# Forward columns of a spectral stage laid end to end in whole PSUM banks

## The chip, the cores and the metric

The kernel runs on one core of one Trainium2 chip. The metric is the device time of one execution in microseconds. Before the change the median of three runs is 1106.13 us (1106.01 to 1106.82). The profiled execution took 1106.58 us, and its span, from the first to the last instruction in the trace, is 1104.8 us.

## The reference, cut to what matters

```python
x  = A_u                                   # (1, 2048, 576)
xn = layernorm(x)
K  = einsum("dn,dnl,dn->dl", Cc, exp(dt*A*l), dt*Bc).real   # response, 576 x 2048
y  = irfft(rfft(xn, padded) * rfft(K, padded))[:2048] + xn * Dskip
out = x + y + silu(xn @ w1) @ w2           # w1: 576 x 4608, w2: 4608 x 576
```

So two branches share the normalised input: a long convolution over 2048 positions with a computed response (done through a transform), and a dense pair of matmuls with a SiLU between them.

## The kernel before, in words

**Dense branch.** `ffn` works in 36 blocks (two halves of the rows, nine chunks of 512 inner features, two blocks of 512 rows). A block has eight main steps: four `up` steps (14 matmuls of 512 columns each, lines 343 to 345) and four `down` steps (24 matmuls of 288 columns, line 369). The operands are split in a high and a low part, so three products stand for one. An `up` result leaves PSUM through ScalarE (`gf`, `gh`, lines 351 and 352) and VectorE (`gl`, line 354). A `down` result is added to `acc` by VectorE (line 373); its bank `po` comes from a pool of two, so a late addition holds up the next `down` step.

**The order of the work.** TensorE, VectorE and ScalarE each run their queue in order. The program gives the dense steps, and a generator `side` gives everything else. `weave` lets the side generator go on whenever the dense branch has reached the share of its 288 main steps that the generator yielded. Where the code says `behind(ins)`, the instructions traced inside come after `ins` on their engine's queue; `tc.high_priority()` puts an instruction ahead of others that are ready. The rest of the order is made by a scheduler when the program is built.

**The spectral stage.** It is the part of `side` between the marks 0.597 and 0.86, main steps 172 to 248, about 671 to 971 us in the trace. Sixteen pairs p of transform rows go through it; each pair has a response side and an input side.

- `load_k(p)`, `load_u(p)`, `load_m(p, i)` (lines 752 to 775) are issued on POOL's queue: the response's rows in five DMAs into `kw`, the input's rows into `u`, and two matrices, `m2` and `mm`. Most tiles have two buffers.
- `halves(p)` (line 777): VectorE's butterfly of the response, three instructions of 128x576 (lines 783 and 785), from `kw` into the tile `k`.
- `visit` (line 787): the forward transform of one side of one pair. Sixteen fp32 matmuls with 64 rows and 32 weight columns, on eight tile positions of the array (two row groups g, four column groups o), each over half of the 576 columns. Every fp32 matmul shows as two instructions, hence x32. The result takes the tile `psb`, four banks with one buffer, and uses 288 of 512 columns in each bank.
- `response(p)` (line 802) is a visit on `k`, a clear of the banks by ScalarE (line 817) and six turns per pair on ScalarE (lines 808 to 810) that make `ka` and `kb`.
- `inputs(p)` (line 819) is a visit on `u`, a clear into `ut`, and the complex product on VectorE: per half two full and two half-height instructions (lines 827 to 830), a cast on ScalarE (`yh`, line 833) and a subtraction on VectorE (`yl`, line 834).
- `back(p)` (line 836): 12 matmuls of 288 columns into the same `psb` tile (line 847), a clear into `yo`, and two stores to `d2` on POOL's queue.

After a start-up the loop at line 877 yields three times for each pair: `response(p+1)`, then `halves(p+2)` and `inputs(p+1)`, then `back(p)`, some 1.4 main steps apart. There are 32 visits and 16 returns. After the stage, `tail` loads the stored rows (`conv_load`, line 933, on SP's queue) and `add_conv` finishes the convolution.

Of the kernel before, what the change touches and what calls it, by code (L numbers as in the profile page):

```python
# [19 lines left out]
P = 128  # L20
L = 2048
D = 576
# [4 lines left out]
HD = D // 2  # L27
# [16 lines left out]
def kernel(  # L44
# [22 lines left out]
    nc = tc.nc  # L67
# [15 lines left out]
    d2 = dram.tile([32 * P, D], F32, name="d2")  # L83
# [66 lines left out]
    pins = {}  # L150

    def behind(ins):
        return tc.issue_after(ins) if ins is not None else nullcontext()
# [306 lines left out]
    kl = yp = pa = tail_at = None  # L460
# [282 lines left out]

    def spectral():

        uv = d1u.rearrange("(m p r) d -> p r m d", m=2, r=P)
        kv = d1k.rearrange("(m p r) d -> p r m d", m=2, r=P)
        cwt = kl.tile([P, 16, 3], F32, name="cwt", bufs=1)
        nc.sync.dma_start(cwt, cw)
        us, ks, mats, kab, ys = {}, {}, {}, {}, {}  # L750

        def load_u(p):
            t = kl.tile([P, 2, D], F32, tag="u", name="u")
            nc.gpsimd.dma_start(t, uv[p])
            us[p] = t

        def load_k(p):
            if p > 15:
                return
            w = kl.tile([P, 3, D], F32, tag="kw", name="kw")  # L760
            nc.gpsimd.dma_start(w[:, 0:2], kv[p])
            for r in range(4):
                nc.gpsimd.dma_start(w[32 * r:32 * r + 32, 2], kv[p, 32 * (r ^ 1):32 * (r ^ 1) + 32, 1])  # L763
            ks[p] = w

        def load_m(p, i):
            if p > 15:
                return
            if i:
                t = kl.tile([P, 2, 2, P], F32R, tag="mm", name="mm")  # L770
                nc.gpsimd.dma_start(t, cm23[:, p, 1:].rearrange("r (k w) c -> r k w c", w=2))
            else:
                t = kl.tile([P, P], F32, tag="m2", name="m2")
                nc.gpsimd.dma_start(t, cm23[:, p, 0])
            mats[p, i] = t

        def halves(p):
            if p > 15:
                return
            w, t = ks[p], kl.tile([P, 2, D], F32, tag="k", name="k", bufs=1)  # L780
            ks[p] = t
            c = cwt[:, p]
            nc.vector.scalar_tensor_tensor(w[:, 2], w[:, 2], c[:, 0:1], w[:, 1], op0=ALU.mult, op1=ALU.add)
            for m in range(2):
                nc.vector.scalar_tensor_tensor(t[:, m], w[:, 2], c[:, 1 + m:2 + m], w[:, 0], op0=ALU.mult, op1=ALU.add)  # L785

        def visit(p, t, name):

            banks = psb.tile([P, 2, 2, 512], F32, tag="psb", name=name)
            last = pins["pe"]  # L790
            for n, (h, g) in enumerate(((0, 1), (0, 0), (1, 1), (1, 0))):
                gs = slice(64 * g, 64 * g + 64)
                for o in range(4):
                    os = slice(32 * o, 32 * o + 32)
                    with tc.high_priority(), behind(last):
                        last = nc.tensor.matmul(banks[os, g, h, :HD], mats[p, 0][gs, os], t[gs, o % 2, h * HD:(h + 1) * HD],
                                                start=True, stop=True, tile_position=(64 * g, 32 * o),
                                                skip_group_check=True).ins
            pins["pe"] = last
            return banks  # L800

        def response(p):

            kas = [kl.tile([P, D], F32, tag="ka", name="ka") for _ in range(2)]
            clear(visit(p, ks.pop(p), "pk"), kas)
            for g in range(2):
                ka, kb = kas[g], kl.tile([P, D], F32, tag="kb", name="kb")
                nc.scalar.mul(kb[:64], ka[64:], -1.0)
                nc.scalar.copy(kb[64:], ka[64:])
                nc.scalar.copy(ka[64:], ka[:64])  # L810
                kab[2 * p + g] = ka, kb

        def clear(banks, dsts):

            with tc.high_priority():
                for g in range(2):
                    nc.scalar.copy(dsts[g].rearrange("p (h d) -> p h d", h=2), banks[:, g, :, :HD])

        def inputs(p):

            uts = [kl.tile([P, D], F32, tag="ut", name="ut") for _ in range(2)]
            clear(visit(p, us.pop(p), "pu2"), uts)
            for g in range(2):
                ka, kb = kab.pop(2 * p + g)
                y = kl.tile([P, D], F32, tag="y", name="y", bufs=1)
                y2 = kl.tile([P, D], F32, tag="y2", name="y2", bufs=1)
                nc.vector.tensor_mul(y, uts[g], ka)  # L827
                nc.vector.tensor_mul(y2[:64], uts[g][64:], kb[:64])
                nc.vector.tensor_mul(y2[64:], uts[g][:64], kb[64:])  # L829
                nc.vector.tensor_add(y, y, y2)  # L830
                ys[2 * p + g] = [kl.tile([P, D], F32R, tag=n, name=n, bufs=2) for n in ("yh", "yl")]
                yh, yl = ys[2 * p + g]
                nc.scalar.copy(yh, y)  # L833
                nc.vector.tensor_sub(yl, y, yh)

        def back(p):

            pb = psb.tile([P, 2, 2, 512], F32, tag="psb", name="pb")
            last = pins["pe"]
            for g in range(2):  # L840
                mk = mats[p, 1][:, g]
                parts = ys.pop(2 * p + g)
# [6 lines left out]
            yos = [kl.tile([P, D], F32, tag="yo", name="yo") for _ in range(2)]  # L849
            clear(pb, yos)  # L850
            for g in range(2):
                nc.gpsimd.dma_start(d2.rearrange("(p k) d -> k p d", k=32)[2 * p + g], yos[g])

        def load_u2(p):
            if p < 16:
                load_u(p)

        load_k(0)
        load_m(0, 0)
        load_u(0)  # L860
        yield 1.0
        with behind(pins["gh"]):
            halves(0)
        load_m(0, 1)
        load_m(1, 0)
        yield 1.03
        load_k(1)
        load_u(1)
        yield 1.05
        response(0)  # L870
        yield 1.07
        halves(1)
        yield 1.085
        inputs(0)
        load_k(2)
        yield 1.1
        for p in range(16):
            if p < 15:
                response(p + 1)
                load_m(p + 1, 1)  # L880
            load_k(p + 3)
            yield 1.1 + 0.9 * (3 * p + 1) / 48
            halves(p + 2)
            if p < 15:
                inputs(p + 1)
            load_u2(p + 2)
            yield 1.1 + 0.9 * (3 * p + 2) / 48
            back(p)
            load_m(p + 2, 0)
            yield 1.1 + 0.9 * (3 * p + 3) / 48  # L890


    order = iter((0, 1, 2, 3, 8, 9, 10, 11, 4, 5, 6, 7, 12, 13, 14, 15))
# [66 lines left out]

    def side():
        nonlocal s4, kl, yp, pa, tail_at, f1, vt, pss, psb, ps3
        marks = (0.13, 0.597, 0.86)
        tail_at = (0.91, 0.934, 0.967, 0.0072)
        with tc.tile_pool(name="kf", bufs=1) as kfp, tc.tile_pool(name="pss", bufs=3, space=PSUM) as pss, tc.tile_pool(name="ps3", bufs=1, space=PSUM) as ps3:
            for n in ("f", "phi"):
# [170 lines left out]
```

## Time and profile before

| | before |
|---|---|
| median of three runs | 1106.13 us |
| profiled execution | 1106.58 us |
| its span | 1104.8 us |
| busy: TensorE, VectorE, ScalarE, POOL | 1095.5, 891.6, 659.5, 136.2 us |
| stage 671 to 971 us: the same | 297.7, 227.8, 199.9, 79.1 us |
| granted TensorE clock in the stage | 1.00 |

The engines are named PE (TensorE's matmuls), PEld (its weight loads, which overlap the matmuls), DVE (VectorE), ACT (ScalarE), POOL (GpSimd) and SP (SyncE). A row of a group reads: line, engine, operation, out<-in, shape, count | busy us, mean ns of one | idle time of the engine just before, and what ended it. A row of a timeline reads: start in us, length in us, engine, line, operation, tiles, shape, count of instructions merged in it. A row of waits reads: who waited for whom, total us, times, longest. Matmuls are pipelined and their ends are modelled, so the starts say how fast TensorE goes on.

### The profile page before, as it was taken

To read this page: it belongs to the slowest core of one execution; us is meant where nothing else is said; L and a number is where in the kernel's file an instruction comes from. 1 tells how busy PE (TensorE), PEld (TensorE's weight loads), DVE (VectorE), ACT (ScalarE), POOL (GpSimd) and SP (SyncE) were. 2 spreads that over 40 slices of the span, in tenths; PEclk is the share of its full clock that TensorE was granted. 3 is DMA by queue.
4 is the path that set the end of the run, shared out by engine and by line. 5 is a ranking of instruction groups with operands and counts; after the bars stand their busy time and mean duration, and the time that the engine had idled before them with its cause. 6 is when DMAs were issued, how large, how long until landed. Compare 5 with 4: busy or idle time off the path is not lost.

```text
span 1104.8 us, 23941 instructions
## 1 busy us (share of the span) xinstructions
PE 1095.5 (99%) x9807; PEld 961.4 (87%) x9807; DVE 891.6 (81%) x1431; ACT 659.5 (60%) x1030; POOL 136.2 (12%) x241
## 2 busy tenths in 40 slices
PE   9999999999999999999999999999999999999998
PEld 7999998999889898999989988788878878899887
DVE  7799899999999999989999836786868768653343
ACT  4565457676776776767766644766666656732220
POOL 1100000000000000011000023323232231000011
PEclk9999999999999999999999999999999999999999
DMA  9745512524253425265754166555546453248563
GB/s 265 208 123 155 150 58 62 121 72 118 85 108 107 99 76 137 62 157 154 198 150 96 55 143 211 163 160 173 166 145 188 151 168 122 67 144 209 135 173 107
DMA packets 174142, 150.23 MB, mean 136 GB/s; under 512 B 112288, under 2 KB 143792, under 8 KB 173904
## 3 DMA queue, kind: packets, MB, share of 16 engines
q1 hardware_dynamic: 156544, 93.77, 32.9%
q0 software_dynamic: 16736, 54.07, 15.6%
q8 instruction: 77, 1.26, 0.5%
q10 hardware_dynamic: 752, 0.85, 0.3%
q14 instruction: 33, 0.27, 0.1%
HBM read 104.13 MB, written 44.61 MB: 135 GB/s over the span
## 4 chain that ended last, share of the span: by engine, by line
PE 80%; DVE 10%; DMA 4%; ACT 2%; POOL 1%; issue 1%; DVEq 0%; ACTq 0%; POOLq 0%
PE po L369 35%; PE ph L343 30%; PE kp L708 3%; DMA kw<-d1k 3%; PE ph L344 3%; PE ph L345 2%; PE z L723 2%; DVE y L829 1%; PE pb L847 1%; DVE y L830 1%; PE pu L171 1%; DVE k L785 1%; DVE acc L373 1%; POOL kw L763 1%; DVE y L827 1%
## 5 line engine op out<-in xcount | busy, mean ns | idle before, releaser
L369 PE MATMUL po<-w2h,gh 128*128 128x288 f32 x1152 | 340.2, 297 | 2.2 <-DVE acc L373 2.1
L369 PE MATMUL po<-w2l,gh 128*128 128x288 f32 x1152 | 337.2, 295 | 0.0
L369 PE MATMUL po<-w2h,gl 128*128 128x288 f32 x1152 | 336.4, 296 | 0.2 <-DVE gl L354 0.2
L369 PEld LDWEIGHTS po<-w2h,gh 128*128 128x128 f32 x1152 | 215.7, 188 | 19.9 <-issue 8.4
L369 PEld LDWEIGHTS po<-w2l,gh 128*128 128x128 f32 x1152 | 215.5, 188 | 6.7 <-issue 1.9
L369 PEld LDWEIGHTS po<-w2h,gl 128*128 128x128 f32 x1152 | 214.9, 188 | 2.9 <-issue 0.9
L351 ACT ACTIVATE gf<-ph 128x512 f32<-128x512 f32 (+1 forms) x146 | 85.8, 588 | 186.9 <-PE ph L345 168.7
L354 DVE TENSOR_TENSOR gl<-gf,gh 128x512 fp32r<-128x512 f32 (+1 forms) x148 | 98.6, 671 | 87.3 <-ACT gh L352 86.7
L373 DVE TENSOR_TENSOR acc<-po,acc 128x288 f32<-128x288 f32 x288 | 126.0, 451 | 47.6 <-PE po L369 46.0
L343 PE MATMUL ph<-xh,w1h 128*128 128x512 f32 (+1 forms) x584 | 159.5, 389 | 0.0
L343 PE MATMUL ph<-xh,w1l 128*128 128x512 f32 (+1 forms) x584 | 159.2, 387 | 0.0
L343 PE MATMUL ph<-xl,w1h 128*128 128x512 f32 (+1 forms) x584 | 159.0, 387 | 0.0
L343 PEld LDWEIGHTS ph<-xl,w1h 128*128 128x128 f32 x584 | 107.0, 188 | 22.0 <-issue 1.4
L343 PEld LDWEIGHTS ph<-xh,w1l 128*128 128x128 f32 x584 | 106.7, 188 | 20.3 <-issue 0.5
L343 PEld LDWEIGHTS ph<-xh,w1h 128*128 128x128 f32 x584 | 103.6, 188 | 17.9 <-issue 0.9
L352 ACT CAST gh<-gf 128x512 fp32r<-128x512 f32 (+1 forms) x148 | 89.3, 610 | 19.4 <-PE po L369 16.4
L174 POOL DMA_DIRECT2D d1u<-u x32 | 17.4, 545 | 462.3 <-ACT u L173 460.4
L667 ACT ACTIVATE c<-th 128x1040 f32<-128x1040 f32 x36 | 38.7, 1075 | 46.0 <-DVE th L666 46.0
L833 ACT CAST yh<-y 128x576 fp32r<-128x576 f32 x32 | 21.5, 673 | 74.2 <-DVE y L830 71.0
L665 ACT ACTIVATE c<-th,magic 128x1040 f32<-128x1040 f32 x36 | 42.1, 1169 | 26.4 <-DVE C L688 23.3
L305 DVE TENSOR_TENSOR w1l<-w1r,w1h 128x640 fp32r<-128x640 f32 x72 | 57.0, 819 | 0.2
L344 PE MATMUL ph<-x,w1h 128*128 128x512 f32 (+1 forms) x146 | 56.6, 388 | 0.0
(195 smaller groups left out, 1757.7 us busy)
## 6 DMA issues: line engine op xcount, KB each, us to landing
w2r<-in_B_w_dram SPq DMA_DIRECT2D x72, 288.0 KB, 3.8
w1r<-in_B_w_dram SPq DMA_DIRECT2D x35, 512.0 KB, 3.9
d1u<-u POOLq DMA_DIRECT2D x32, 288.0 KB, 3.0
d1k<-stage SPq DMA_DIRECT2D x36, 256.0 KB, 5.1
u<-d1u POOLq DMA_DIRECT2D x16, 576.0 KB, 4.6
kw<-d1k POOLq DMA_DIRECT2D x16, 576.0 KB, 4.6
d<-yo POOLq DMA_DIRECT2D x32, 288.0 KB, 3.0
ys<-d SPq DMA_DIRECT2D x32, 288.0 KB, 6.0
```

The source lines that it names most:

```text
L305: pins["w1l"] = nc.vector.tensor_sub(l1, src, h1).ins
L343: nc.tensor.matmul(ph, w[:, kt, :], v[:, kt, a:e], start=n + kt == 0, stop=False)
L344: nc.tensor.matmul(ph, h1[:, 4, :], x4[:, a:e], start=False, stop=False)
L345: pins["pe"] = nc.tensor.matmul(ph, l1[:, 4, :], x4[:, a:e], start=False, stop=True).ins
L351: nc.scalar.activation(gf, ph, AF.Silu)
L352: pins["gh"] = nc.scalar.copy(gh, gf).ins
L354: pins["gl"] = nc.vector.tensor_sub(gl, gf, gh).ins
L369: pins["pe"] = nc.tensor.matmul(po[:, :HD], G[blk, t][g][:, js], W2[half, c, t][w][:, hs], start=n == 0, stop=n == 3 * FT - 1).ins
L373: nc.vector.tensor_add(acc[j][:, hs], po[:, :HD], acc[j][:, hs])
L665: nc.scalar.activation(c65, th, AF.Identity, bias=magic)
L667: nc.scalar.activation(c65, th, AF.Abs)
L708: mm = nc.tensor.matmul(dst, t[:, ch, :32], t[:, ch, 32:], start=begins and n == 0, stop=True, tile_position=(0, 32 * q), skip_group_check ...
```

## The change

The 32 visits of 576 columns become 18 visits that fill all four banks. All forward columns are numbered end to end in the order k0, u0, k1, u1, and so on (k the response side of a pair, u its input side, 576 columns each, for both row groups). Visit v takes the columns 1024 v to 1024 v + 1023; a piece ends where its side or its bank ends. That makes 64 pieces, eight each of 64, 128, 192, 256, 320, 384, 448 and 512 columns, three or four of them in most visits. Within a visit the matmuls take the response's pieces first, the newest pair first. Each piece is cleared by one ScalarE copy for both row groups.

`products(p)` holds the turns and the complex product. It is emitted right after the visit in which the input side of p ends; the turns come there too, no longer after the response's visit. The products are made in place (`ut`, `kb`), the butterfly in place in `kw`, so `k`, `y` and `y2` go; `ka` and `ut` have room for two pairs, `m2` for three.

`halves(p)` has a place of its own: in the visit after the one that frees its `kw` tile, at the latest in the visit before its first use. For the four pairs where these coincide (6, 7, 14 and 15, "tight"), and where no return is pending (pairs 2 and 10), it stands behind the sum of the products just emitted; else behind the last `yl` of the visit before.

`back(p)` follows the visit after the one in which p ended, and `load_m(p+1, 1)` comes after it instead of before. The stage now reaches to 0.876 of the main steps. With 34 steps for visits and returns, a visit and the return after it are each some 2.2 main steps from the next; the visits 1 and 2, counted from 0, and 10 and 11 have no return between them. Counted so, the third visit is visit 2 and the twelfth is visit 11.

```diff
+        visits = [[] for _ in range((2 * D * NP + 1023) // 1024)]
+        for p in range(NP):
+            for kind in range(2):
+                c, at = 0, 2 * D * p + D * kind
+                while c < D:
+                    n = min(D - c, 512 - (at + c) % 512)
+                    visits[(at + c) // 1024].append((kind, p, c, n, (at + c) % 1024 // 512, (at + c) % 512))
+                    c += n
...
-            w, t = ks[p], kl.tile([P, 2, D], F32, tag="k", name="k", bufs=1)
-            nc.vector.scalar_tensor_tensor(w[:, 2], w[:, 2], c[:, 0:1], w[:, 1], op0=ALU.mult, op1=ALU.add)
-            for m in range(2):
-                nc.vector.scalar_tensor_tensor(t[:, m], w[:, 2], c[:, 1 + m:2 + m], w[:, 0], op0=ALU.mult, op1=ALU.add)
...
+                nc.vector.scalar_tensor_tensor(w[:, 2], w[:, 2], c[:, 0:1], w[:, 1], op0=ALU.mult, op1=ALU.add)
+                for m in range(2):
+                    nc.vector.scalar_tensor_tensor(w[:, 1 - m], w[:, 2], c[:, 1 + m:2 + m], w[:, 0],
+                                                   op0=ALU.mult, op1=ALU.add)
...
-            for n, (h, g) in enumerate(((0, 1), (0, 0), (1, 1), (1, 0))):
+            for kind, p, c, n, b, at in sorted(visits[v], key=lambda piece: (piece[0], -piece[1])):
+                for g in (1, 0):
+                    gs = slice(64 * g, 64 * g + 64)
+                    for o in (1, 0, 3, 2):
...
+                            last = nc.tensor.matmul(banks[os, g, b, at:at + n], mats[p, 0][gs, os], src[:, c:c + n],
...
+            for kind, p, c, n, b, at in visits[v]:
...
+                with tc.high_priority():
+                    nc.scalar.copy(held[p][:, :, c:c + n], banks[:, :, b, at:at + n])
...
+        for v in range(len(visits)):
+            yield 1.07 + (2 - 1.07) * n / steps
+            n += 1
+            visit(v)
+            for kind, p in ends[v]:
+                if kind:
+                    load_u(p + 2)
+                    load_m(p + 3, 0)
+                else:
+                    load_k(p + 2)
+            done = [p for kind, p in ends[v] if kind]
+            was = pins.get("yl")
+            for p in done:
+                for _ in products(p):
+                    pass
+            for p in due.get(v, ()):
+                if not done:
+                    yield 1.07 + (2 - 1.07) * (n - 0.4) / steps
+                with behind(pins["sum"] if done and (p in tight or not ready) else was if ready else pins["gl"]):
+                    halves(p)
+            for p in ready:
+                yield 1.07 + (2 - 1.07) * n / steps
+                n += 1
+                back(p)
                 load_m(p + 1, 1)
...
-        marks = (0.13, 0.597, 0.86)
+        marks = (0.13, 0.597, 0.876)
```

More of the change, by code (lines that the diff above doesn't have):

```diff
@@ L744, in spectral @@
     def spectral():
+        NP = 16
         uv = d1u.rearrange("(m p r) d -> p r m d", m=2, r=P)
         kv = d1k.rearrange("(m p r) d -> p r m d", m=2, r=P)
-        cwt = kl.tile([P, 16, 3], F32, name="cwt", bufs=1)
+        cwt = kl.tile([P, NP, 3], F32, name="cwt", bufs=1)
         nc.sync.dma_start(cwt, cw)
-        us, ks, mats, kab, ys = {}, {}, {}, {}, {}
+        us, ks, mats, kas, uts, ys = {}, {}, {}, {}, {}, {}
+        visits = [[] for _ in range((2 * D * NP + 1023) // 1024)]
[6 more added lines that the diff above has]
+                    c += n
@@ L752, in load_u @@
+        ends = [[(kind, p) for kind, p, c, n, _, _ in v if c + n == D] for v in visits]
         def load_u(p):
-            t = kl.tile([P, 2, D], F32, tag="u", name="u")
-            nc.gpsimd.dma_start(t, uv[p])
-            us[p] = t
+            if p < NP:
+                us[p] = kl.tile([P, 2, D], F32, tag="u", name="u")
+                nc.gpsimd.dma_start(us[p], uv[p])
         def load_k(p):
-            if p > 15:
-                return
-            w = kl.tile([P, 3, D], F32, tag="kw", name="kw")
@@ L761, in load_k @@
[L761 to L764, printed above, removed]
-        def load_m(p, i):
[L767 to L775, printed above, removed]
@@ L777, in halves @@
-        def halves(p):
-            if p > 15:
-                return
-            w, t = ks[p], kl.tile([P, 2, D], F32, tag="k", name="k", bufs=1)
-            ks[p] = t
-            c = cwt[:, p]
-            nc.vector.scalar_tensor_tensor(w[:, 2], w[:, 2], c[:, 0:1], w[:, 1], op0=ALU.mult, op1=ALU.add)
-            for m in range(2):
-                nc.vector.scalar_tensor_tensor(t[:, m], w[:, 2], c[:, 1 + m:2 + m], w[:, 0], op0=ALU.mult, op1=ALU.add)
-        def visit(p, t, name):
-            banks = psb.tile([P, 2, 2, 512], F32, tag="psb", name=name)
-            last = pins["pe"]
-            for n, (h, g) in enumerate(((0, 1), (0, 0), (1, 1), (1, 0))):
[L792 to L798, printed above, removed]
-            pins["pe"] = last
-            return banks
@@ L802, in response @@
-        def response(p):
-            kas = [kl.tile([P, D], F32, tag="ka", name="ka") for _ in range(2)]
-            clear(visit(p, ks.pop(p), "pk"), kas)
-            for g in range(2):
[L807 to L817, printed above, removed]
@@ L819, in inputs @@
-        def inputs(p):
-            uts = [kl.tile([P, D], F32, tag="ut", name="ut") for _ in range(2)]
-            clear(visit(p, us.pop(p), "pu2"), uts)
-            for g in range(2):
[L824 to L834, printed above, removed]
+            if p < NP:
+                w = ks[p] = kl.tile([P, 3, D], F32, tag="kw", name="kw")
+                nc.gpsimd.dma_start(w[:, 0:2], kv[p])
+                for r in range(4):
+                    nc.gpsimd.dma_start(w[32 * r:32 * r + 32, 2], kv[p, 32 * (r ^ 1):32 * (r ^ 1) + 32, 1])
@@ new lines, in load_m @@
+        def load_m(p, i):
+            if p < NP:
+                if i:
+                    t = kl.tile([P, 2, 2, P], F32R, tag="mm", name="mm")
+                    nc.gpsimd.dma_start(t, cm23[:, p, 1:].rearrange("r (k w) c -> r k w c", w=2))
+                else:
+                    t = kl.tile([P, P], F32, tag="m2", name="m2", bufs=3)
+                    nc.gpsimd.dma_start(t, cm23[:, p, 0])
+                mats[p, i] = t
+        def halves(p):
+            if p < NP:
+                w, c = ks[p], cwt[:, p]
+                nc.vector.scalar_tensor_tensor(w[:, 2], w[:, 2], c[:, 0:1], w[:, 1], op0=ALU.mult, op1=ALU.add)
+                for m in range(2):
+                    nc.vector.scalar_tensor_tensor(w[:, 1 - m], w[:, 2], c[:, 1 + m:2 + m], w[:, 0],
+                                                   op0=ALU.mult, op1=ALU.add)
@@ new lines, in visit @@
+        def visit(v):
+            banks = psb.tile([P, 2, 2, 512], F32, tag="psb", name="pf")
+            last = pins["pe"]
+            for kind, p, c, n, b, at in sorted(visits[v], key=lambda piece: (piece[0], -piece[1])):
+                for g in (1, 0):
+                    gs = slice(64 * g, 64 * g + 64)
+                    for o in (1, 0, 3, 2):
+                        os = slice(32 * o, 32 * o + 32)
+                        src = us[p][gs, o % 2] if kind else ks[p][gs, 1 - o % 2]
+                        with tc.high_priority(), behind(last):
+                            last = nc.tensor.matmul(banks[os, g, b, at:at + n], mats[p, 0][gs, os], src[:, c:c + n],
+                                                    start=True, stop=True, tile_position=(64 * g, 32 * o),
+                                                    skip_group_check=True).ins
+            pins["pe"] = last
+            for kind, p, c, n, b, at in visits[v]:
+                held, tag = (uts, "ut") if kind else (kas, "ka")
+                if c == 0:
+                    held[p] = kl.tile([P, 2, D], F32, tag=tag, name=tag)
+                with tc.high_priority():
+                    nc.scalar.copy(held[p][:, :, c:c + n], banks[:, :, b, at:at + n])
@@ new lines, in products @@
+        def products(p):
+            ut, ka = uts.pop(p), kas.pop(p)
+            kb = kl.tile([P, 2, D], F32, tag="kb", name="kb", bufs=1)
+            for g in range(2):
+                nc.scalar.mul(kb[:64, g], ka[64:, g], -1.0)
+                nc.scalar.copy(kb[64:, g], ka[64:, g])
+                nc.scalar.copy(ka[64:, g], ka[:64, g])
+            yield
+            for g in range(2):
+                nc.vector.tensor_mul(kb[:64, g], ut[64:, g], kb[:64, g])
+                nc.vector.tensor_mul(kb[64:, g], ut[:64, g], kb[64:, g])
+                nc.vector.tensor_mul(ut[:, g], ut[:, g], ka[:, g])
+                added = nc.vector.tensor_add(ut[:, g], ut[:, g], kb[:, g]).ins
+                if not g:
+                    pins["sum"] = added
+                yh, yl = (kl.tile([P, D], F32R, tag=n, name=n) for n in ("yh", "yl"))
+                nc.scalar.copy(yh, ut[:, g])
+                pins["yl"] = nc.vector.tensor_sub(yl, ut[:, g], yh).ins
+                ys[p, g] = yh, yl
+            yield
@@ L841, in back @@
                 mk = mats[p, 1][:, g]
-                parts = ys.pop(2 * p + g)
+                parts = ys.pop((p, g))
                 for h in range(2):
@@ L848, in back @@
             pins["pe"] = last
-            yos = [kl.tile([P, D], F32, tag="yo", name="yo") for _ in range(2)]
-            clear(pb, yos)
+            yo = kl.tile([P, 2, D], F32, tag="yo", name="yo", bufs=1)
             for g in range(2):
[L852 to L856, printed above, removed]
+                with tc.high_priority():
+                    nc.scalar.copy(yo[:, g].rearrange("p (h d) -> p h d", h=2), pb[:, g, :, :HD])
+                nc.gpsimd.dma_start(d2.rearrange("(p k) d -> k p d", k=32)[2 * p + g], yo[:, g])
         load_k(0)
@@ L863, in spectral @@
             halves(0)
+        load_k(1)
+        load_m(1, 0)
+        load_u(1)
         load_m(0, 1)
[L865 to L871, printed above, removed]
-        halves(1)
[L873 to L879, printed above, removed]
-                load_m(p + 1, 1)
[L881 to L887, printed above, removed]
+        yield 1.04
+        halves(1)
+        load_m(2, 0)
+        steps = len(visits) + NP
+        n = 0
+        ready = []
+        due, tight = {}, []
+        for p in range(2, NP):
+            freed = (2 * D * (p - 2) + D - 1) // 1024
+            due.setdefault(min(freed + 1, 2 * D * p // 1024 - 1), []).append(p)
+            if 2 * D * p // 1024 - 1 == freed:
+                tight.append(p)
+        for v in range(len(visits)):
[6 more added lines that the diff above has]
+                    load_m(p + 3, 0)
+                else:
+                    load_k(p + 2)
[13 more added lines that the diff above has]
+                back(p)
+                load_m(p + 1, 1)
+            ready = done
+        for p in ready:
+            yield 1.07 + (2 - 1.07) * n / steps
+            n += 1
             back(p)
-            load_m(p + 2, 0)
-            yield 1.1 + 0.9 * (3 * p + 3) / 48
+        yield 2
     order = iter((0, 1, 2, 3, 8, 9, 10, 11, 4, 5, 6, 7, 12, 13, 14, 15))
```

## The prediction, on record before the changed kernel ran

> **What bounds the kernel now.** I read the page first: span, engines, chain.
>
> ```profile
> span 1104.8 us, 23941 instructions
> PE 1095.5 (99%) x9807; PEld 961.4 (87%) x9807; DVE 891.6 (81%) x1431; ACT 659.5 (60%) x1030; POOL 136.2 (12%) x241
> PE 80%; DVE 10%; DMA 4%; ACT 2%; POOL 1%; issue 1%; DVEq 0%; ACTq 0%; POOLq 0%
> ```
>
> TensorE is busy for 1095.5 of 1104.8 us and carries 80% of the chain, so time comes off only where TensorE does less or waits less. The changed stage, about 671 to 971 us, stands in the stretch view (columns: PE, PEld, DVE, ACT, POOL, clock), and what TensorE waits for there in the view of waits.
>
> ```profile
> 671.00:971.00 300.00, 297.65 (x2569) 246.91 (x2568) 227.80 (x351) 199.94 (x330) 79.11 (x142) 1.00 0.49 151
> ```
>
> ```profile
> PE po L369 <- DVE acc L373: 2.1, 3, 0.7
> ```
>
> Only 2.1 of 300 us are named waits, at full clock. No wait is worth removing; what remains is the time that the visits themselves occupy. So next the timeline of TensorE, around one visit (second matrix: without one):
>
> ```profile
> 706.57 1.07 PE L343 MATMUL ph<-xl,w1h 128*128 128x512 f32 x4
> 707.57 1.20 PE L796 MATMUL pk<-k,m 64*32 64x288 f32 x32
> 708.70 1.20 PE L343 MATMUL ph<-xh,w1l 128*128 128x512 f32 x4
> 709.74 0.39 PE L344 MATMUL ph<-x,w1h 128*128 128x512 f32 x1
> ```
>
> ```profile
> 717.20 1.07 PE L343 MATMUL ph<-xl,w1h 128*128 128x512 f32 x4
> 718.11 1.07 PE L343 MATMUL ph<-xh,w1l 128*128 128x512 f32 x4
> 719.01 0.39 PE L344 MATMUL ph<-x,w1h 128*128 128x512 f32 x1
> ```
>
> Eight dense matmuls take 719.01 - 717.20 = 1.81 us (0.226 each). With a visit among them they take 709.74 - 706.57 = 3.17. **A visit costs 1.36 us.** How much of that is columns? The same timeline, cut off at 707.83, 708.07 and 708.31:
>
> ```profile
> 707.57 0.47 PE L796 MATMUL pk<-k,m 64*32 64x288 f32 x8
> ...
> 707.57 0.71 PE L796 MATMUL pk<-k,m 64*32 64x288 f32 x16
> ...
> 707.57 0.96 PE L796 MATMUL pk<-k,m 64*32 64x288 f32 x24
> ```
>
> The 32 instructions start in waves of eight (one for each of eight array tiles), and each further wave lengthens the stretch by 0.24 us. Four waves (two passes of fp32, two halves of 288) are 0.97 us, so 576 columns cost 1.69 ns a column. The other **0.39 us is fixed**: a gap before, the run-out of the last wave, the restart of the dense stream (709.74 - 708.70 is 1.04, not 0.91).
>
> **The change, part by part.**
>
> *Fewer visits.* 32 visits of 576 columns become 18 of 1024; columns are the same 18432, the instructions too (64 pieces of 16, where there were 64 halves of 16). Before: 32 x 1.36 = 43.5 us. After: 18 x (1024 x 1.69 ns + 0.39) = 18 x 2.12 = 38.2. That is 14 x 0.39 = **-5.4 us**. No other engine covers or shares this time: TensorE is the bound and in order.
>
> *Uneven pieces.* Pieces now have 64 to 512 columns, eight of each size of 64, 128 and so on. By columns a piece of 64 takes 0.108 us. The nearest short matmuls are those of the response's table product:
>
> ```profile
> 408.69 0.34 PE L708 MATMUL kp<-C 128*32 128x64 f32 x8
> 408.83 0.32 PE L708 MATMUL kp<-S 128*32 128x64 f32 x8
> 408.94 0.32 PE L708 MATMUL kp<-C 128*32 128x64 f32 x7
> 409.05 0.22 PE L708 MATMUL kp<-S 128*32 128x64 f32 x1
> ```
>
> 23 of 64 columns start in 0.36 us, 16 ns each, on four tiles. At that pace 16 take 0.25: 0.14 too much for each of eight pieces of 64, 0.03 for each of 128, so 0 to 1.4 us in all. I take **+0.5**, nearer zero, since eight tiles instead of four share the stream here.
>
> *VectorE, ScalarE.* Counts per pair stay: ten products and three butterfly steps on VectorE, two clears' worth of elements, six turns and two casts on ScalarE. The rows, over the stage:
>
> ```profile
> L785 DVE SCALAR_TENSOR_TENSOR k<-kw,cwt 128x576 f32<-128x576 f32 x32 | 24.7, 812 | 0.0
> L828 DVE TENSOR_TENSOR y<-ut,kb 64x576 f32<-64x576 f32 x32 | 24.0, 750 | 1.4
> L808 ACT ACTIVATE kb<-ka 64x576 f32<-64x576 f32 x32 | 21.9, 684 | 0.8
> L817 ACT COPY ut<-pu 128x576 f32<-128x576 f32 x32 | 18.8, 639 | 0.3 <-PE pu L796 0.3
> ```
>
> A pair is 10 x 0.75 + 3 x 0.81 = 9.9 us of VectorE before and after, in place or not (full and half-height products differ little; the row of line 827 stands below). Zero, as long as the order holds (below).
>
> *The fixed place.* The butterfly now sits behind a sum or the last `yl`, and each visit starts with the rows it made, so TensorE waits at the visit's head. Behind that head stand all dense matmuls. At visits 2 and 11 (counted from 0) only two main steps pass since the visit before: 28 x 0.226 = 6.3 us. Chain: clear of the last input piece (at most 0.64), four products to the sum (3.0), butterfly (2.4): 6.1, or 7.5 with the dense work's own additions between. Late by 0 to 1.3; if the three turns (2.0) come after the clear as well, 3.3. Twice: 0 to 6.6 us. The turns need only the earlier visit's columns and ScalarE is 67% busy, so I lean to the low end: **+0.6** in all.
>
> *Loads.* `load_k` follows the visit that frees its tile. Rows of the transfers, and the landings of the u and kw tiles in turn:
>
> ```profile
> L763 POOL DMA_DIRECT2D kw<-d1k x64 | 31.8, 504 | 2.2 <-DMA u<-d1u 0.7 <-DMA kw<-d1k 0.6 <-DVE acc L373 0.6
> L761 POOL DMA_DIRECT2D kw<-d1k x16 | 11.5, 721 | 83.8 <-DVE k L785 82.4 <-DMA kw<-d1k 1.4
> ```
>
> ```profile
> DMA to landing us min/median/max: 4.2/4.6/8.6
> ...
> DMA to landing us min/median/max: 3.1/4.2/9.4
> ```
>
> At the four tight pairs (6, 7, 14, 15): five issues 2.7 + landing 4.2 + butterfly 2.4 = 9.3 us, against four main steps, 56 x 0.226 = 12.7. Covered by 3.4 us; with the longest landing late by 1.8. The input load at visits 2 and 11 (4.6) has 6.3 us and the first 576 columns. Zero. `load_m(p+1, 1)` moves behind `back(p)`, so POOL no longer sits on its tile's release ahead of `load_k`. That helps loads, which TensorE does not wait for.
>
> *The later end.* The last `back` moves from main step 246.3 to 250.1, about 13 us. Its store and the first loads of what it stores (POOL, SP), and the page's row of the store's landing:
>
> ```profile
> 978.03 1.08 POOL L852 DMA_DIRECT2D d<-yo  x2 [6.58 <-ACT yo L817]
> ```
>
> ```profile
> 998.75 1.27 SPq L933 DMA_DIRECT2D ys<-d  x2
> ```
>
> ```profile
> d<-yo POOLq DMA_DIRECT2D x32, 288.0 KB, 3.0
> ```
>
> 978 + 13 + 1 + 3 = 995, before 998.8. Zero; without that cover the loads, not TensorE, slip by the excess.
>
> **Sum:** -5.4 + 0.5 + 0.6 = -4.3, on the profiled execution's 1106.58 us (span 1104.8 and 1.8 around it): 1102.3. The median of the runs shown is 1106.13, 0.45 lower: **1101.8**.
>
> The Trainium skill speaks against the short pieces: "TensorE: Matmul & The Clock Gate", section "Back-to-back issue gap", gives matmuls of 1 to 64 columns an issue floor of about 25 ns. By the Trainium skill's figure, as an estimate, 16 matmuls never take under 0.40 us, and the pieces of 64, 128 and 192 would lose about 4.4 us together; the sum would be about 1105.7. The trace disagrees: 16 ns each at 64 columns on line 708.
>
> **Rivals.**
>
> *The dense stream is starved (slower).* VectorE is in order. Where products stack up ahead of an addition that frees a bank, TensorE stops, as here (VectorE, then TensorE):
>
> ```profile
> 699.01 0.81 DVE L783 SCALAR_TENSOR_TENSOR kw<-kw,cwt 128x576 f32<-128x576 f32 x1
> 699.74 0.75 DVE L827 TENSOR_TENSOR y<-ut,ka 128x576 f32<-128x576 f32 x1
> 700.50 0.75 DVE L828 TENSOR_TENSOR y<-ut,kb 64x576 f32<-64x576 f32 x1
> 701.27 0.76 DVE L829 TENSOR_TENSOR y<-ut,kb 64x576 f32<-64x576 f32 x1
> 702.05 0.82 DVE L373 TENSOR_TENSOR acc<-po,acc 128x288 f32<-128x288 f32 x2
> ```
>
> ```profile
> 701.26 0.63 PE L343 MATMUL ph<-xl,w1h 128*128 128x512 f32 x2
> 702.57 0.40 PE L369 MATMUL po<-w2h,gh 128*128 128x288 f32 x1 [0.67 <-DVE acc L373]
> ```
>
> Start to start 0.85 us is lost. Before has three of these. The change emits a pair's products as one body and ties the butterfly to it; that makes such stacks likelier. With ten more the time is 1101.8 + 8.5 = 1110. Slower by 0.2% (1108.3) from eight more on. Against it: VectorE is idle 72 of 300 us, and the butterfly no longer waits for its transfer ahead of others.
>
> *Visits come late or in parts (no change).* The first visit now is torn:
>
> ```profile
> 671.77 0.67 PE L796 MATMUL pk<-k,m 64*32 64x288 f32 x2
> ...
> 673.29 1.20 PE L796 MATMUL pk<-k,m 64*32 64x288 f32 x30
> ```
>
> Each tear costs another 0.39 us; a visit with several sources can be torn more easily, and fourteen tears undo the gain. Ten, or both close visits at 3.3 us late, give about 1105.5. Against: starting with the newest rows makes the rest ready.
>
> *Short waves show their weight loads (no change).*
>
> ```profile
> L796 PEld LDWEIGHTS pk<-k,m 64*32 64x32 f32 x512 | 7.9, 106 | 7.5 <-issue 3.6 <-DVE kw L783 0.4 <-ACT gh L352 0.4
> ```
>
> A weight load lasts 0.106 us and now lies under a wave of 0.24. If it stands in the open wherever a piece has under 256 columns (24 pieces, two waves each), that is 48 x 0.106 = 5.1 us where I have 0.5: 1106.4. Against it: line 708 starts a matmul every 16 ns, with a load for each.
>
> *All waits go (faster).* If the three late additions of the stage vanish too (2.6 us), without the +0.6 and +0.5: 1106.1 - 5.4 - 2.6 = 1098.1.
>
> **How the numbers follow.** A measurement of this kernel can tell about 0.2% (2.2 us). Forecast with its spread down to 1098: 0.58, the bare faster end below it 0.04. Late or torn visits 0.13, weight loads 0.04: 0.17 for no change. Starved stream 0.21. So faster 0.62, same 0.17, slower 0.21. The range takes in all waits gone (1098) and ten more stalls (1110); beyond them lie about 0.04 and 0.1.
>
> **What would show it.** 18 groups of forward matmuls of some 2.1 us each, and fixed gaps of 0.39 at each; their sum near 38 instead of 43.5 us. Line 373's waits in TensorE's list staying near 2 to 3 us; ten and more mean the starved stream. A wait for a butterfly or clear at the visits' heads, above all the third and the twelfth, means late visits; more than 18 groups, torn ones. I would be wrong if a visit of 1024 columns took much over 2.1 us, or VectorE's order changed for the worse.

## The result, and the profile after

The changed kernel takes 1099.24 us (median of 6 runs, 1099.05 to 1099.32); the kernel before took 1106.47 us beside it (1105.44 to 1107.43). The ratio is 0.9934, 95% interval 0.9921 to 0.9947. The forecast was 1101.8 us in a range from 1098 to 1110. The span of the profiled execution went from 1104.8 to 1097.4 us, by 7.4. Further down, each run's ratio is to the kernel before, run beside it; its distance to the changed kernel is one between medians of different sessions, in which the kernel before stood between 1105.77 and 1106.47.

The page's first lines after the change, and the shares of the chain by engine:

```profile
span 1097.4 us, 23933 instructions
PE 1090.0 (99%) x9807; PEld 963.2 (88%) x9807; DVE 888.0 (81%) x1431; ACT 658.9 (60%) x1030; POOL 136.6 (12%) x241
PE 98%; DVE 1%; DMA 0%; issue 0%; POOL 0%; ACTq 0%; DVEq 0%; ACT 0%
```

TensorE executes the same 9807 matmuls in 5.5 us less busy time, and the chain that was 80% TensorE and 10% VectorE is now 98% TensorE. The same stretch of the stage as before:

```profile
671.00:971.00 300.00, 300.00 (x2618) 256.65 (x2618) 226.33 (x353) 202.47 (x334) 78.37 (x141) 1.00 0.50 151
```

The profile shows no gap of TensorE in these 300 us, where it was busy for 297.65, and 2618 matmuls are counted in them instead of 2569. The view of TensorE's waits for 640 to 990 us is empty. VectorE's own waits there:

```profile
DVE acc L373 <- PE po L369: 61.0, 31, 4.9
...
DVE kw L788 <- DMA kw<-d1k: 2.5, 1, 2.5
```

And in the kernel before, from 640 to 970 us:

```profile
DVE acc L373 <- PE po L369: 13.2, 11, 3.9
...
DVE kw L783 <- DMA kw<-d1k: 11.6, 5, 5.4
```

So additions now wait for TensorE 31 times, 61 us in all, instead of 11 times, and TensorE no longer waits for any of them. The butterfly waits for its load once instead of five times. The wait that is left, 2.5 us, ends at 669.29, ahead of the first visit; the kernel before has the same one there, 2.86 us.

Now two visits of the changed kernel in TensorE's timeline. The first is visit 4, two pieces of 512 columns; the second, visit 3, has pieces of 128, 448, 64 and 384 (rows that follow each other on one line and tile are merged, with the first shape shown).

```profile
729.05 0.84 PE L343 MATMUL ph<-xl,w1h 128*128 128x512 f32 x3
729.82 1.09 PE L804 MATMUL pf<-kw,m 64*32 64x512 f32 x16
730.70 1.06 PE L804 MATMUL pf<-u,m 64*32 64x512 f32 x16
731.70 0.40 PE L369 MATMUL po<-w2h,gh 128*128 128x288 f32 x1
731.93 0.29 PE L369 MATMUL po<-w2l,gh 128*128 128x288 f32 x1
```

```profile
714.26 0.40 PE L344 MATMUL ph<-x,w1h 128*128 128x512 f32 x1
714.59 1.20 PE L804 MATMUL pf<-kw,m 64*32 64x128 f32 x32
715.58 1.12 PE L804 MATMUL pf<-u,m 64*32 64x64 f32 x32
716.64 0.40 PE L369 MATMUL po<-w2h,gh 128*128 128x288 f32 x1
716.87 0.29 PE L369 MATMUL po<-w2l,gh 128*128 128x288 f32 x1
```

Undisturbed, three dense matmuls from 729.05 and one of 288 columns (0.13) would have brought the second `po` matmul to 729.86. It came at 731.93: visit 4 cost 2.07 us. In the same way visit 3 cost 716.87 - 714.26 - 0.23 - 0.13 = 2.25 us. All ten visits without a piece of 64 columns cost 2.07 to 2.09, all eight with one 2.24 to 2.26. So the visits take 10 x 2.09 + 8 x 2.25 = 38.9 us, against 32 x 1.34 = 42.9 (measured in the same way; 1.33 to 1.36) and 0.8 more because the first one was torn: 4.8 us less. With the three late additions, 2.6, that is 7.4, as large as the change of the span.

The sum leaves out smaller stops that nearly cancel. The kernel before has some 0.9 us of them, around 811 and 893 us. The changed kernel has a new one, just behind the stretch for which the view of waits is empty:

```profile
998.13 0.29 PE L369 MATMUL po<-w2h,gl 128*128 128x288 f32 x1
998.43 0.94 PE L369 MATMUL po<-w2h,gh 128*128 128x288 f32 x3
...
999.88 0.29 PE L369 MATMUL po<-w2h,gl 128*128 128x288 f32 x1
```

From 998.13 to 999.88 eight matmuls start in 1.75 us, where 8 x 0.13 = 1.05 would do: 0.7 lost.

### The profile page after: what moved, and what is told of

It is laid out like the page before. It is cut to its first block, busy times and chain, and to the rows that moved or that the text cites. A ratio compares the mean times of both kernels' runs of the same rounds, so it can differ in the third digit from the quotient of the medians.

```text
span 1097.4 us, 23933 instructions
## 1 busy us (share of the span) xinstructions
PE 1090.0 (99%) x9807; PEld 963.2 (88%) x9807; DVE 888.0 (81%) x1431; ACT 658.9 (60%) x1030; POOL 136.6 (12%) x241
## 4 chain that ended last, share of the span: by engine, by line
PE 98%; DVE 1%; DMA 0%; issue 0%; POOL 0%; ACTq 0%; DVEq 0%; ACT 0%
PE po L369 42%; PE ph L343 36%; PE kp L708 3%; PE pf L804 3%; PE ph L345 3%; PE ph L344 3%; PE pb L848 2%; PE z L723 2%; PE pu L171 1%; PE py L963 1%; PE pu L172 1%; PE pt L134 0%; DMA acc<-in_A_u_dram 0%; DVE w1l L305 0%; DVE st L203 0%; PE ptk L502 0%
## 5 line engine op out<-in xcount | busy, mean ns | idle before, releaser
L345 PE MATMUL ph<-x,w1l 128*128 128x512 f32 (+1 forms) x146 | 56.7, 389 | 0.0
```

The source lines that it names most:

```text
L345: pins["pe"] = nc.tensor.matmul(ph, l1[:, 4, :], x4[:, a:e], start=False, stop=True).ins
```

## The experiments

Theory A: a visit has a fixed cost on TensorE, that of leaving the dense shape of the array (128x128) for the tiles of 64x32 and coming back, and the butterfly's place in VectorE's queue took away the late additions. Theory B: the gain came from the wider spread of the stage or from the new products and buffers.

**The spread alone.** In the kernel before:

```diff
-        marks = (0.13, 0.597, 0.86)
+        marks = (0.13, 0.597, 0.876)
```

> The kernel before with only the mark of the stage's end moved from 0.86 to 0.876. Theory A, with the late additions of VectorE gone through the order of its queue and not through more room: 1105.5 to 1107, as before. Theory B, the wider spread alone makes VectorE's additions come in time: the 2.6 us of late additions go, 1103.5 to 1104.

1106.74 us, ratio to before 1.0007 (0.9998 to 1.0015). The spread alone brings nothing: the trace still shows two late additions.

**The spread taken back from the changed kernel.** The same line the other way round.

> The changed kernel with the stage's end put back from 0.876 to 0.86 of the main steps, so 16 pairs have 6 per cent less room. Theory A, the order of VectorE's queue removed the late additions: within 0.7 us of the changed kernel, 1099 to 1100, no addition late in the stage. Theory B, the room did: two or three additions late again by 0.85 us, 1101 to 1102.

1100.83 us, ratio 0.9955 (0.9943 to 0.9968), 1.6 us more than the changed kernel. Both theories missed the time. No addition is late, as theory A had it, and 1.5 us of the excess lie at one point, where the last return leaves the stage and a dense step waits for ScalarE's clear of that return. TensorE's timeline there:

```profile
972.77 0.29 PE L848 MATMUL pb<-yh,mm 128*128 128x288 f32 x1
974.38 0.40 PE L369 MATMUL po<-w2h,gh 128*128 128x288 f32 x1 [1.31 <-ACT yo L853]
```

So the order holds in less room too; the new mark buys the end of the stage, not its middle.

**The butterfly left free.** In the changed kernel:

```diff
-                with behind(pins["sum"] if done and (p in tight or not ready) else was if ready else pins["gl"]):
-                    halves(p)
+                halves(p)
```

> The changed kernel with the butterfly left free in VectorE's queue (no instruction named that it must follow). Theory P, the fixed place keeps it from waiting for its load ahead of additions: two to four additions late again by 0.85 us, 1101 to 1102.6 us, with VectorE's waits for the kw load back near 10 us. Theory Q, the place does not matter for TensorE: 1099.2.

1102.88 us, ratio 0.9970 (0.9959 to 0.9980), 3.6 more than the changed kernel, and the runs scatter again (1101.9 to 1104.33). TensorE's waits, then one of VectorE's:

```profile
PE po L369 <- DVE acc L373: 1.5, 2, 0.8
PE po L369 <- DVE gl L354: 1.1, 1, 1.1
```

```profile
DVE kw L788 <- DMA kw<-d1k: 11.6, 6, 2.5
```

That is the picture of before, in the new structure. The visits also stand in 20 groups instead of 18, because two are torn. The place matters, as theory P said (its range ended 0.3 us lower).

Why it matters is less clear. The expectation blames the wait for the load, but the two late additions hold TensorE up until 697.84 and 701.47, and the nearest wait for a load ended at 681.90, 16 us earlier. In the kernel before it is alike: the first late addition, at 702.05 in VectorE's list, has no wait for a load near it, and the other two, at 821.78 and 898.71, come 8.5 us after waits of 0.79 and 1.25 us. So these runs show that the butterfly's place decides; that the wait for its load is the reason, they do not show.

**The place in the old structure, first try.** In the kernel before:

```diff
-            halves(p + 2)
             if p < 15:
                 inputs(p + 1)
+            with behind(pins["yl"]):
+                halves(p + 2)
```

> The kernel before with one edit: the butterfly of pair p+2 is emitted after the products of pair p+1 and follows their last subtraction in VectorE's queue, 32 visits as before. Theory A, the place alone takes away the late additions: their 2.6 us go, 1103.5 to 1104. Theory B, they go only with the new products and buffers: 1105.5 to 1107, as before.

1173.77 us, ratio 1.0614 (1.0599 to 1.0628): a miss of both sides. The butterfly of pair p+2 now follows the products of pair p+1, and those need the response's columns, turned by ScalarE, of the visit before. In TensorE's queue the last visits and returns stand one behind the other, from 967 to 1043 us, with the remaining dense matmuls only behind them (the first at 1044.57), so the chain shows bare. TensorE, then the rows of VectorE that close it:

```profile
985.73 2.69 PE L796 MATMUL pk<-k,m 64*32 64x288 f32 x32 [6.69 <-DVE k L785]
989.80 2.17 PE L796 MATMUL pu<-u,m 64*32 64x288 f32 x32 [1.38 <-ACT ka L817]
995.04 0.61 PE L847 MATMUL pb<-yh,mm 128*128 128x288 f32 x1 [3.07 <-ACT ut L817]
...
1004.97 2.69 PE L796 MATMUL pk<-k,m 64*32 64x288 f32 x32 [6.68 <-DVE k L785]
```

```profile
994.48 0.76 DVE L827 TENSOR_TENSOR y<-ut,ka 128x576 f32<-128x576 f32 x1 [8.28 <-ACT ut L817]
...
1003.05 0.81 DVE L783 SCALAR_TENSOR_TENSOR kw<-kw,cwt 128x576 f32<-128x576 f32 x1
1003.90 1.55 DVE L785 SCALAR_TENSOR_TENSOR k<-kw,cwt 128x576 f32<-128x576 f32 x2
```

One pair takes 1004.97 - 985.73 = 19.2 us in series: visit, clear, six turns, clear, products, subtraction, butterfly, next visit. The stage has 300 us for 16 pairs, 18.8 for each, and beside dense work the same steps also stand in queues. The first and the last of ten response visits there are 235.7 us apart, 26 us for a pair:

```profile
711.37 1.20 PE L796 MATMUL pk<-k,m 64*32 64x288 f32 x30
...
947.11 1.19 PE L796 MATMUL pk<-k,m 64*32 64x288 f32 x30
```

So the place has to be one that VectorE reaches earlier.

**The place in the old structure, second try.** The butterfly stays where it was emitted and follows the last subtraction of pair p, one pair earlier:

```diff
-            halves(p + 2)
+            with behind(pins["yl"]):
+                halves(p + 2)
             if p < 15:
                 inputs(p + 1)
```

> The kernel before, 32 visits, with one edit: the butterfly of pair p+2, emitted where it was, now follows the last subtraction of the pair before (pair p) in VectorE's queue, a point that is long past. It no longer closes the chain from products to butterfly to visit that took 19 us for a pair when it stood behind pair p+1. Theory A, a place that the butterfly cannot run ahead of takes the late additions away in the old structure too: their 2.6 us go, 1103.3 to 1104. Theory B, they go only together with the new buffers and the later products: 1105 to 1107, as before.

1103.30 us, ratio 0.9977 (0.9968 to 0.9986), 2.5 below the 1105.77 of before beside it, with a spread of 0.4 us where before has 2.6. TensorE waits for no addition, and VectorE's butterfly waits for its load once:

```profile
DVE kw L783 <- DMA kw<-d1k: 2.8, 1, 2.8
```

At the spot of the first late addition the list of VectorE now reads:

```profile
698.47 0.45 DVE L373 TENSOR_TENSOR acc<-po,acc 128x288 f32<-128x288 f32 x1
...
701.15 0.46 DVE L373 TENSOR_TENSOR acc<-po,acc 128x288 f32<-128x288 f32 x1
```

In the kernel before, the stage's fourth butterfly starts at 699.01 and stands, with three products, ahead of both additions, which come at 702.05. Here it starts at 708.01, behind them. What changes at this spot is the order in the queue.

Theory A: one constraint on one instruction's place is worth 2.5 us in the old structure. Buffers and products are not needed for it. And with the late additions gone from both structures, 1103.30 and 1099.24 are 4.1 us apart: what the visits bring, 4.8 by their rows, less the 0.7 lost behind 998 us.

**32 visits in the new structure.** The table of visits is replaced, and with it the visit in which a butterfly is due; the rest is as changed:

```diff
+        visits = [[(kind, p, 0, HD, 0, 0), (kind, p, HD, HD, 1, 0)] for p in range(NP) for kind in range(2)]
...
+            due.setdefault(2 * p - 3, []).append(p)
```

> The changed kernel, but with 32 visits of 576 columns (two pieces of 288) in place of 18 of 1024; clears, products, order rules and marks as changed. Theory A, a fixed cost of each visit: 14 visits more at 0.37 to 0.39 us are +5.3, and the eight pieces of 64 columns that go take back 1.2, so +4.1 on the changed kernel, about 1103.3 us. Theory B, the order and the spread brought the gain: within 0.7 us of the changed kernel, 1099 to 1100.

1130.27 us, ratio 1.0207 (1.0193 to 1.0221): a miss of both. The visits that stand among dense matmuls cost 1.33 to 1.35 us each, as before. But the return of a pair now is to follow its input visit by 3.1 main steps instead of 4.4, and the last visits are left over at the end, in series:

```profile
993.30 1.21 PE L797 MATMUL pf<-kw,m 64*32 64x288 f32 x32 [1.34 <-ACT ut L806]
999.33 0.61 PE L841 MATMUL pb<-yh,mm 128*128 128x288 f32 x1 [4.82 <-ACT yh L825]
```

It is the same kind of chain as in the run at 1173.77 us; that the nearer return makes it is argued here, not shown. The edit also moves the butterflies: by the rule of the changed kernel all fourteen from pair 2 on now stand behind the sum just emitted, where the changed kernel has six there. As a test of the fixed cost the time decides nothing, so the next run adds that cost without touching the order.

**One switch more in each visit.** In the changed kernel, ahead of a visit's last piece:

```diff
+                if (kind, p, c, n, b, at) == order_v[-1]:
+                    with tc.high_priority(), behind(last):
+                        last = nc.tensor.matmul(banks[:, 0, b, at:at + 64], ident, ident[:, :64], start=True, stop=True,
+                                                skip_group_check=True).ins
```

> The changed kernel with one full-array fp32 matmul of 64 columns put ahead of the last piece of each of the 18 visits, on columns of the visit's banks that the piece then overwrites; its product is used by nothing. Its own columns cost 0.11 us by the 1.69 ns a column of the visits. Theory A, the fixed cost of a visit is that of going from one shape of the array to the other and back: 18 x (0.38 + 0.11) = +8.8, about 1108 us. Theory C, the fixed cost belongs to the dense stream's stop and restart only: 18 x 0.11 = +2, about 1101.2.

1107.58 us, ratio 1.0016 (1.0007 to 1.0025): 8.3 us more than the changed kernel, 0.46 for each visit, where theory A had 0.49. Visit 4 in its timeline:

```profile
731.84 1.09 PE L809 MATMUL pf<-kw,m 64*32 64x512 f32 x16
732.86 0.43 PE L801 MATMUL pf<-ident 128*128 128x64 f32 x2
733.22 1.09 PE L809 MATMUL pf<-u,m 64*32 64x512 f32 x16
```

From the first piece's start to the second's are 1.38 us, in the changed kernel 730.70 - 729.82 = 0.88. Of the 0.50 between, 0.11 are the estimate for its columns; 0.39 are left for going from tiles to the full array and back, with no dense stream involved. That is the fixed cost of a visit again, and theory C is out by 6 us. One rival is not excluded by this run: the piece behind the added matmul writes the same columns of the bank, and may wait for them. A visit among dense matmuls shares no bank with them and has the same fixed cost, which speaks against it.

**Newest rows last.** In the changed kernel:

```diff
-            for ... in sorted(visits[v], key=lambda piece: (piece[0], -piece[1])):
+            for ... in sorted(visits[v], key=lambda piece: (-piece[0], piece[1])):
```

> The changed kernel, but each visit takes the input side and the oldest pair first and the newest rows last. In TensorE's queue this gives 24 groups of forward matmuls instead of 18, since the scheduler lets dense matmuls in where the newest rows are not ready. Theory A, each group has a fixed cost of 0.38 us: 6 x 0.38 = +2.3, about 1101.5, and more where TensorE then waits for a butterfly inside a visit. Theory B, groups cost nothing by themselves: 1099.2 to 1099.5.

1100.38 us, ratio 0.9952 (0.9939 to 0.9964): 1.1 more than the changed kernel, with 24 groups in the trace. The sign is that of theory A, the time half of it. Two of the groups make up visit 2, 10 us apart:

```profile
688.74 0.99 PE L804 MATMUL pf<-u,m 64*32 64x256 f32 x32
698.75 1.20 PE L804 MATMUL pf<-kw,m 64*32 64x256 f32 x32
```

They cost 1.12 and 1.33 us, 2.45 together against 2.09 in one: 0.36 for the tear. Six visits are torn, so the tears come to 2.2 us, and TensorE waits 0.4 us for a butterfly. Against that, four visits no longer pay 0.16 for a piece of 64 columns that now stands first or last (visit 0 among them: torn for only 0.2), and the 0.7 us behind 998 us do not occur. That adds up to 1.3, near the 1.1 measured. So beginning with the newest rows is worth about 1 us, mostly by keeping visits whole.

**Short pieces last.** In the changed kernel:

```diff
-            for ... in sorted(visits[v], key=lambda piece: (piece[0], -piece[1])):
+            for ... in sorted(visits[v], key=lambda piece: (piece[3] < 128, piece[0], -piece[1])):
```

> The changed kernel with the pieces of 64 columns at the end of their visits. Theory S, the 0.15 us that each visit with such a piece takes longer is a supply of instructions that runs dry behind it, shown by the next wave's starts 17 ns apart instead of 7: with dense matmuls behind, which need one instruction pair in 131 ns, it goes: 8 x 0.15 = -1.2, about 1098.0 us. Theory T, the short piece itself costs it: no change, 1099.2.

1098.28 us (1097.87 to 1098.39), ratio 0.9924 (0.9912 to 0.9937): 0.96 below the changed kernel, theory S. Visit 3, to be held against the one above:

```profile
714.05 0.40 PE L344 MATMUL ph<-x,w1h 128*128 128x512 f32 x1
714.38 1.20 PE L804 MATMUL pf<-kw,m 64*32 64x128 f32 x32
715.37 0.96 PE L804 MATMUL pf<-u,m 64*32 64x384 f32 x32
716.27 0.40 PE L369 MATMUL po<-w2h,gh 128*128 128x288 f32 x1
716.50 0.29 PE L369 MATMUL po<-w2l,gh 128*128 128x288 f32 x1
```

716.50 - 714.05 - 0.36 = 2.09 us, where it was 2.25. Of all the versions run here this is the fastest.

## Why the prediction was right, and where it was off

The sign, the main term and the range held; the forecast of 1101.8 lies 2.6 us above the result. The range held because its lower end took in the rival in which all waits go; the sum itself had not counted that.

- **Fewer visits, -5.4.** Measured -5.3: 42.9 for 32 visits and 18 x 2.09 = 37.6 without the short pieces' surcharge. The two sizes of visit alone give the same split: (2.08 - 1.34) / 448 columns is 1.65 ns a column, which leaves 0.39 of 1.34. The switch in the middle of a visit priced it at 0.39 too.
- **Uneven pieces, +0.5.** Mis-sized: +1.3, 0.16 for each of eight pieces, at the upper end that line 708 gave (0.14). The reason that I gave for leaning to zero, eight tiles sharing the stream, was the wrong one to look at: the short piece itself runs at full pace, the piece behind it pays (last section).
- **The fixed place, +0.6.** Zero, but by luck. No wait for a butterfly or a clear stands at any visit's head, the third and twelfth included, and the turns ran ahead of the clear, as assumed. Yet the working had two numbers wrong that cancel. TensorE left visit 1 at 681.64, and VectorE started the last instruction of the butterfly for visit 2 at 694.26:

```profile
681.64 0.40 PE L369 MATMUL po<-w2h,gl 128*128 128x288 f32 x1
...
698.07 1.20 PE L804 MATMUL pf<-kw,m 64*32 64x256 f32 x32
```

```profile
694.26 0.80 DVE L790 SCALAR_TENSOR_TENSOR kw<-kw,cwt 128x576 f32<-128x576 f32 x1
```

From the clear (682.17) to the butterfly's end the chain took 12.9 us, not 6.1 to 7.5, because other work of VectorE stood in between. And visit 2 started not 6.3 but 16.4 us behind visit 1. At 6.3 it would have waited some 7 us; the order made when the program was built had put more dense work ahead of it. Visit 11 came 17 us behind visit 10.

- **VectorE's order, zero.** This is the step that failed by most. I counted instructions, found them equal, and left the three late additions standing; their end I put down as a rival's edge (1098.1). The place of the butterfly takes them away, as the free butterfly (back by 3.6) and the old kernel with one constraint (2.5 less) show. I had the new place as an argument only against the slow rival, because the butterfly no longer waits for its transfer ahead of others; that this wait made the additions late is not shown (see the run with the butterfly left free).
- **The torn first visit, 0.8,** stood in a quoted row, and I counted it for the rival alone, not as a part of what goes.
- **Loads, the later end:** zero, as costed. The view of waits is empty. The last store is issued at 981.29 instead of 978.03, 3.3 us later and not 13, and the first load of what was stored goes out on SP's queue at 1001.26.
- **The late starts behind 998 us, 0.7,** no term had.

Counted from the forecast, that is -2.6, -0.8 and -0.6 for the late additions, the torn visit and the fixed place, and +0.8 and +0.7 for the short pieces and the late starts: -2.5 of the 2.6 us.

The starved stream did not come. VectorE's products are emitted as one body, but the scheduler spread them, and in the stage additions wait for TensorE, not the other way. It does come when the butterfly is set free, with 1.5 us of named waits. Bare weight loads did not come either: visits with pieces of 128 columns cost no more than those of 512.

## What to carry to other kernels

Where TensorE is full, count how often it changes between array shapes, and price one change from two rows of its timeline. Letting columns wait until they fill whole banks can then cost less than going at once, with more visits. The place of one instruction in the queue of an engine that works in order can decide over the bound engine's waits. An instruction that needs a load belongs behind work that ends after the load has landed, but well ahead of the step that uses its result: one such constraint brought 2.5 us here, and the same constraint one pair later closed a chain of 19 us. Short tiled matmuls belong at the end of a group, or at its head, but not in its middle.

## What the runs showed of the hardware that was not expected

**Behind a short piece in the middle of a visit the tiles start slowly.** TensorE's timeline of the changed kernel from the piece of 64 columns on, cut at 715.75, 715.85 and 715.89:

```profile
715.58 0.59 PE L804 MATMUL pf<-u,m 64*32 64x64 f32 x17
...
715.58 0.77 PE L804 MATMUL pf<-u,m 64*32 64x64 f32 x22
...
715.58 0.80 PE L804 MATMUL pf<-u,m 64*32 64x64 f32 x24
```

The 16 short matmuls and one more start within 0.17 us; the next seven come after a pause and need until 715.89, some 17 ns each, where the tiles of other waves start 7 ns apart. With dense matmuls behind, one in 131 ns, the surcharge goes. It also goes when the short piece comes first. Visit 8 of the run with the newest rows last begins with the piece of 64 columns:

```profile
799.03 0.85 PE L343 MATMUL ph<-xl,w1h 128*128 128x512 f32 x3
799.82 1.20 PE L804 MATMUL pf<-u,m 64*32 64x64 f32 x32
...
802.03 1.09 PE L343 MATMUL ph<-xh,w1l 128*128 128x512 f32 x4
```

With four dense matmuls in these 3.00 us it cost 3.00 - 4 x 0.23 = 2.08, like a visit without a short piece. So it is not the short piece alone that slows the next one, but a short piece behind other tiles. A store of weight and matmul instructions that is full behind dense work, and refills at some 17 ns a pair, would fit; whether that is it, the runs do not show.

The Trainium skill ("TensorE: Matmul & The Clock Gate", section "Back-to-back issue gap") gives matmuls of 1 to 64 columns an issue floor of about 25 ns. The trace of these tiled matmuls does not agree: starts lie 7 ns apart in most waves and 17 behind the short piece.

**A starved TensorE is slow when work comes.** In the run at 1173.77 us a visit after a wait of 6.69 us lasted 2.69 instead of 1.20 us, and the granted clock of that stretch was 0.59:

```profile
967.00:1030.00 63.00, 26.80 (x292) 14.57 (x292) 30.43 (x41) 29.34 (x47) 12.80 (x23) 0.59 0.29 90
```

So here a chain that leaves TensorE empty for microseconds costs twice, and the 67 us lost in that run are not all waiting.
